# Gradient factors with all tokens in one row, one transposing load per block, key and value spectra in one load, and a new order

## The chip, the cores and the metric

The kernel runs on one core of a Trainium2 chip. The metric is device time in microseconds, the median of repeated executions. A separate execution was recorded by the profiler; its rows are what the text quotes. Engines are named as the profile names them: PE is TensorE's matmuls, PEld its weight loads, DVE is VectorE, ACT is ScalarE, POOL is GpSimd, and SP (SPq) is SyncE, which issues nearly all of the DMAs here.

## The reference

What is computed is the output of a block and all of its gradients. The input `q` (2048 tokens, 512 features, bf16) is normalised per token; the normalised rows feed two branches that are multiplied and added to the input.

```python
def _A_ref(q, k, v, shift_k, ssm_k, ssm_D):      # 4-tap shift, gate, long convolution by FFT
    for t in range(ks):
        k_shift = k_shift + k_pad[:, t:t + S, :] * shift_k[:, ks - 1 - t][None, None, :]
    kv = k_shift * v
    y = irfft(rfft(pad(kv)) * rfft(pad(ssm_k)))[:S] + kv * ssm_D
    return q * y

def _B_ref(x, w_gate, w_up, w_down):             # gated unit, F = 1376
    h = _sigmoid(x @ w_gate) * (x @ w_up)
    return h @ w_down

xn = _layernorm(A_q)
out = A_q + _A_ref(xn, ...) * _silu(_B_ref(xn, ...))
# returned: out, and the vjp with grad_out for q, k, v, shift_k, ssm_k, ssm_D, w_gate, w_up, w_down
```

(The FFT line is shortened to its meaning.) The outputs are `out_0` (the result), `out_1` to `out_6` (gradients of q, k, v, shift_k, ssm_k, ssm_D) and `out_7` to `out_9` (gradients of w_gate, w_up, w_down).

## The kernel before, in words

All data is bf16 with sums in f32. Tokens are cut into 16 tiles of 128 (`NJ`), taken in 8 pairs (`NP`); features into 4 groups of 128 (`NG`); the hidden size is padded to 11 blocks of 128 (`NFB`). The transforms of length 4096 are matmuls with tables (`step1`, `flip`, `step2` forward, `inv2`, `inv1` back), so a spectrum is a tile of 128 x 2048.

The work consists of generators, called streams here. The forward ones normalise (`f_ln`), compute gate and up products (`strG`), the spectra of the filter (`strK`) and of the gated input (`strV`, `strX`), and the rest of the gated unit (`strZ`). `strD` computes the gradient of the hidden layer. Three factors that the weight gradients need go to device memory on the way, through the helper `fm`: `hD` (the hidden layer h), `dgD` and `duD` (the gradients at the gate and up products), each stored feature by feature with tokens along the row. The spectra of the filter and of the gated input go to `KD` and `VD`, one 128 x 2048 tile for each group and half.

In the last part three streams run together. `dW` makes the weight gradients in 18 blocks: for each of the three factors, five blocks of 256 hidden features and one of 96. A block's operand is a tile `L` of 128 x 16 x 256 (token within a tile, tile, feature), read back from device memory by a transposing DMA in `ld_L`. Three such tiles take turns (`L_r`): after a block has been computed, `ld_L` asks for the block three further on. `frontC` and `backC` carry the gradient back through the convolution; `ld_KV` brings the two spectra in again, which `backC` multiplies by the gradient's spectrum, and the next two are asked for at the same place, so two pairs of tiles take turns. `last_rows` writes the two smallest gradients from a corner of one of these tiles.

Nothing is issued as the streams produce it. A recorder (`Rec`) collects all operations with a number each, and `emit` issues them in an order written out by hand: the table `ORDER` has one list of numbers for each engine's queue and one, `moves`, for the order of the DMAs over all queues, and `BANKS` says which PSUM banks each accumulator takes. As all operations pass through one line of `emit`, the profile shows line L524 for all of them, and they are told apart by engine, operation, tile name and shape. Buffers in SBUF come from one slab (`Arena`, `Ring`), so the profile calls every SBUF operand `slab`; the names of device memory (`KD`, `VD`, `hD`, `dgD`, `duD`) stay visible. A DMA in SP's queue waits there until what it reads is written and what it overwrites has been read, and everything behind it in that queue waits too.

Of the kernel before, what the change touches and what calls it, by code (L numbers as in the profile page):

```python
# [12 lines left out]
bf16 = mybir.dt.bfloat16  # L13
# [3 lines left out]
P = 128  # L17
NFFT = 4096
SCALE_INV = 2.0 / NFFT
S = 2048  # L20
# [3 lines left out]
NJ = 16  # L24
NFB = 11
LN_EPS = 1e-5
NG = 4
GW = D // NG
# [622 lines left out]
def kernel_impl(ctx, tc, A_q, A_k, A_v, A_shift_k, A_ssm_k, A_ssm_D, B_x, B_w_gate, B_w_up, B_w_down,  # L651
                grad_out, out_0, out_1, out_2, out_3, out_4, out_5, out_6, out_7, out_8, out_9):
    nc = tc.nc
# [12 lines left out]
    def fm(dst, p):  # L666
        o = 256 * (p % 4)
        return dst[p // 4][:, :, o:o + 256].rearrange("f p t -> p f t")
# [3 lines left out]
    ar = Arena(slab, SLAB)  # L672
# [879 lines left out]
```

## Time and profile before

| | |
|---|---|
| median of 3 runs | 447.37 us (446.88 to 447.51) |
| profiled execution | 446.62 us |
| its span in the profile | 444.3 us |
| PE busy | 433.5 us (98%), 4,871 matmuls recorded |
| DVE busy | 409.9 us (92%) |
| ACT busy | 279.8 us (63%) |
| POOL busy | 21.8 us (5%) |
| granted TensorE clock, mean | 0.997 |
| DMA moved | 116.85 MB, 263 GB/s on average |

Times within the span count from its start. Busy time is not work at full rate: matmuls overlap, so the mean length of one (the ns in the groups) is more than what it adds to a run of them; for that the busy time of a group is divided by its count. A DMA has two times: how long the issuing engine was occupied, and when its last byte landed. Rows with an arrow say what an engine waited for; the name behind the arrow is the releaser that came last. In rows of SPq the time is SP's own.

### The profile page before, as it was taken

How to read it: one execution, taken by the hardware profiler on the slowest of the kernel's cores; microseconds unless marked ns; L12 is line 12 of the kernel's file. 1: busy time of each engine (PE TensorE's matmuls, PEld its weight loads, DVE VectorE, ACT ScalarE, POOL GpSimd, SP SyncE). 2: the span in 40 equal slices, each digit the busy share in tenths (PEclk: the TensorE clock that was granted, in tenths of full speed). 3: DMA queues.
4: the chain of work that ended last, by engine and by line, in shares of the span. 5: the costliest groups of instructions: out<-in, count | busy, mean ns of one | idle time of the engine just before them, and what ended most of it. 6: DMA issues, size and time to landing. Idle time of an engine off the chain costs nothing.

```text
span 444.3 us, 11521 instructions
## 1 busy us (share of the span) xinstructions
PE 433.5 (98%) x4871; PEld 303.7 (68%) x4907; DVE 409.9 (92%) x630; ACT 279.8 (63%) x351; POOL 21.8 (5%) x48
## 2 busy tenths in 40 slices
PE   8999999999999999999999999999999999999994
PEld 3886686677868677655656655445577887887883
DVE  8899999999979898999999897899899999999991
ACT  7998878789777658786425333354556754656522
POOL 8301000001000000000000000000000000000000
PEclk9999999999999999999999999999999999999998
DMA  8999899779188999999899999799999999999998
GB/s 273 328 360 258 202 345 345 229 268 318 69 245 245 248 230 266 265 327 316 281 246 337 289 239 272 224 270 257 243 236 285 218 236 255 236 223 251 277 257 248
DMA packets 195813, 116.85 MB, mean 263 GB/s; under 512 B 107130, under 2 KB 182450, under 8 KB 195634
## 3 DMA queue, kind: packets, MB, share of 16 engines
q1 hardware_dynamic: 194688, 115.72, 99.2%
q8 instruction: 38, 0.62, 0.6%
q10 hardware_dynamic: 1074, 0.39, 0.3%
q14 instruction: 13, 0.11, 0.1%
HBM read 43.87 MB, written 46.70 MB: 204 GB/s over the span
## 4 chain that ended last, share of the span: by engine, by line
PE 94%; DVE 2%; issue 1%; DMA 1%; POOL 0%; ACT 0%; DVEq 0%
PE psum L524 94%; DVE slab L524 2%; DMA slab<-in_A_q_dram 1%; POOL slab L524 0%; ACT slab L524 0%; DVEq L524 0%
## 5 line engine op out<-in xcount | busy, mean ns | idle before, releaser
L524 PE MATMUL psum<-slab 128*128 128x256 bf16 (+5 forms) x4871 | 433.5, 299 | 4.6 <-DVE slab L524 1.9
L524 PEld LDWEIGHTS <-slab 128*128 128x128 bf16 (+2 forms) x4907 | 303.7, 96 | 134.2 <-issue 30.1
L524 ACT CAST slab<-psum 128x1024 bf16<-128x1024 f32 (+3 forms) x224 | 192.0, 897 | 128.6 <-PE psum L524 112.7
L524 DVE TENSOR_TENSOR slab<-slab 128x1024 bf16<-128x1024 bf16 (+4 forms) x302 | 239.9, 832 | 7.3 <-ACT slab L524 4.1
L524 DVE STREAM_TRANSPOSE slab<-slab 128x1024 f32<-128x1024 f32 x48 | 64.5, 1357 | 2.6 <-ACT slab L524 1.8
L524 ACT ACTIVATE slab<-slab 128x512 bf16<-128x512 bf16 (+5 forms) x59 | 49.5, 879 | 23.9 <-DVE slab L524 23.7
L524 DVE CAST slab<-psum 128x1024 bf16<-128x1024 f32 (+3 forms) x29 | 31.4, 1089 | 5.6 <-PE psum L524 5.2
L524 DVE TENSOR_TENSOR slab<-psum,slab 128x512 bf16<-128x512 f32 (+2 forms) x52 | 31.7, 610 | 3.4 <-PE psum L524 1.9
L524 ACT ACTIVATE slab<-psum 128x512 bf16<-128x512 f32 (+1 forms) x48 | 27.0, 575 | 2.0 <-PE psum L524 1.9
L524 POOL MEMSET slab<- 128x128 bf16 (+3 forms) x10 | 4.5, 453 | 273.1 <-PE psum L524 141.2
L524 DVE SCALAR_TENSOR_TENSOR slab<-slab 128x2 f32<-128x2 f32 (+2 forms) x41 | 14.3, 358 | 1.0 <-POOL slab L524 0.8
L524 POOL TENSOR_TENSOR slab<-slab 128x2 f32<-128x2 f32 (+3 forms) x11 | 11.1, 1016 | 77.5 <-DVE slab L524 77.4
L524 ACT ACT_TABLE_LOAD x10 | 12.8, 1283 | 1.9 <-issue 1.8
L524 DVE SCALAR_TENSOR_TENSOR slab<-psum,slab 128x512 bf16<-128x512 f32 x16 | 10.8, 684 | 3.3 <-PE psum L524 3.3
L524 DVE BATCH_NORM_STATS2 slab<-slab 128x6 f32<-128x512 bf16 x16 | 10.7, 677 | 0.9 <-DMA slab<-in_A_q_dram 0.9
L524 DVE STREAM_SHUFFLE slab<-slab 128x1024 f32<-128x1024 f32 x8 | 10.6, 1320 | 0.0
L524 ACT COPY slab<-psum 128x512 bf16<-128x512 bf16 (+2 forms) x10 | 7.4, 755 | 2.6 <-PE psum L524 2.6
L524 DVE TENSOR_SCALAR slab<-slab 128x512 bf16<-128x512 bf16 (+6 forms) x30 | 8.4, 299 | 0.1
L524 DVE COPY slab<-psum 128x512 bf16<-128x512 bf16 (+1 forms) x9 | 4.6, 526 | 0.2 <-PE psum L524 0.2
L524 POOL TENSOR_SCALAR slab<-slab 128x1 f32<-128x1 f32 (+3 forms) x10 | 3.3, 331 | 0.5
L524 DVE MEMSET slab<- 32x192 uint32 (+3 forms) x10 | 1.5, 160 | 1.3 <-PEq L1536 0.9
L524 DVE BATCH_NORM_AGGREGATE slab<-slab 128x2 f32<-128x6 f32 x16 | 2.5, 166 | 0.0
(14 smaller groups left out, 9.2 us busy)
## 6 DMA issues: line engine op xcount, KB each, us to landing
slab<-KD SPq DMA_DIRECT2D x16, 512.0 KB, 5.2
out_dram<-slab SPq DMA_DIRECT2D x31, 256.0 KB, 3.6
hD<-slab SPq DMA_DIRECT2D x8, 704.0 KB, 5.0
duD<-slab SPq DMA_DIRECT2D x8, 704.0 KB, 5.5
dgD<-slab SPq DMA_DIRECT2D x8, 704.0 KB, 5.2
slab<-in_A_k_dram SPq DMA_DIRECT2D x4, 1024.0 KB, 6.4
KD<-slab SPq DMA_DIRECT2D x8, 512.0 KB, 4.9
VD<-slab SPq DMA_DIRECT2D x8, 512.0 KB, 5.0
```

What stands on the lines that cost most here:

```text
L524: getattr(getattr(self.nc, eng), meth)(*[place(v) for v in a], **{x: place(v) for x, v in k.items()})
```

## The change

Three things change.

1. `hD`, `dgD` and `duD` were each two tensors of 11 x 128 x 1024 (feature block, feature, tokens of one half); each is now one of 11 x 128 x 2048. `ld_L` read a block by two transposing DMAs of 256 x 1024, one for each half of the tokens; it now reads it by one of 256 x 2048. 36 transposing loads of blocks become 18.
2. `KD` and `VD` become one tensor `KVD` with K and V side by side, 4 KB each, per partition. The two stores stay two, and `ld_KV` brings both in by one DMA of 128 x 4096 into one tile (`KV_r`). 16 loads become 8. The row-swapped read in `swap` takes the new pitch.
3. `ORDER` and `BANKS` are new tables: the recorder's numbers change with the removed DMAs (6,144 operations before, 6,118 now), and the order of the rest on every engine is another one. The set of matmuls, by shape and number, is the same.

```diff
-    KD = [dram.tile([2, P, 2048], bf16, name=f"KD{g}") for g in range(NG)]
-    VD = [dram.tile([2, P, 2048], bf16, name=f"VD{g}") for g in range(NG)]
+    KVD = [dram.tile([2, P, 2, 2048], bf16, name=f"KVD{g}") for g in range(NG)]
...
-    hD, dgD, duD = ([dram.tile([NFB, P, 1024], bf16, name=f"{t}{h}") for h in range(2)] for t in ("hD", "dgD", "duD"))
+    hD, dgD, duD = (dram.tile([NFB, P, S], bf16, name=t) for t in ("hD", "dgD", "duD"))
 
     def fm(dst, p):
-        o = 256 * (p % 4)
-        return dst[p // 4][:, :, o:o + 256].rearrange("f p t -> p f t")
+        return dst[:, :, 256 * p:256 * p + 256].rearrange("f p t -> p f t")
...
-                nc.sync.dma_start(KD[cg][q], KF)
+                nc.sync.dma_start(KVD[cg][q, :, 0], KF)
...
-            K = KD[n // 2][n % 2]
-            nc.sync.dma_start(KS, bass.AP(K.tensor, K.offset + 2048, [[4096, 64], [-2048, 2], [1, 2048]]))
+            K = KVD[n // 2][n % 2]
+            nc.sync.dma_start(KS, bass.AP(K.tensor, K.offset + 4096, [[8192, 64], [-4096, 2], [1, 2048]]))
...
-                nc.sync.dma_start(VD[cg][q], Xc)
+                nc.sync.dma_start(KVD[cg][q, :, 1], Xc)
...
         nb = 2 if u < 5 else 1
-        for h in range(2):
-            nc.sync.dma_start_transpose(L[:, 8 * h:8 * h + 8, 0:128 * nb], srcs[s][h][2 * u:2 * u + nb].rearrange("f p t -> (f p) t"))
+        nc.sync.dma_start_transpose(L[:, :, 0:128 * nb], srcs[s][2 * u:2 * u + nb].rearrange("f p t -> (f p) t"))
...
-            KK, VV = KK_r.next(), VV_r.next()
-            nc.sync.dma_start(KK, KD[cg][q])
-            nc.sync.dma_start(VV, VD[cg][q])
-            stC["KV", n] = KK, VV
+            KV = KV_r.next()
+            nc.sync.dma_start(KV, KVD[cg][q])
+            stC["KV", n] = KV[:, 0], KV[:, 1]
...
 ORDER = {
     "sync": """
...
-        5378 5597 5595 4775 5734 5234 5735 4576 5926 5733 4772 5925 5927 5965 5757 6006 6143 6075 5921 6008 6109 5825
-        5918
+        5710 5213 5572 5709 4561 5901 5900 4756 5732 5800 5980 5896 6049 6117 5982 6083 5939 5893
```

Three places show how the order moved. In its rows a name with an arrow is what an instruction writes and reads, a shape is that of what it writes, and a count at the end stands for equal neighbours. A transposing load of 128x8x256 is half a block, one of 128x16x256 a whole one; `slab<-in_A_k_dram` is the key's halves and their 3-row borders for the backward part.

First place: SP's queue in the last third, where blocks of `duD` are loaded beside the stores. Before:

```order
L524 DMA_TRANSPOSE slab<-duD_98 128x8x256
L524 DMA out_dram<-slab 128x4x256 x2
L524 DMA slab<-KD_64 128x2048
L524 DMA_TRANSPOSE slab<-duD_97 128x8x256
L524 DMA out_dram<-slab 128x2048
L524 DMA_TRANSPOSE slab<-duD_98 128x8x256
L524 DMA_TRANSPOSE slab<-duD_97 128x8x256
L524 DMA_TRANSPOSE slab<-duD_98 128x8x256
L524 DMA slab<-VD_68 128x2048
L524 DMA out_dram<-slab 128x4x96
L524 DMA_TRANSPOSE slab<-duD_97 128x8x256
```

and now:

```order
L520 DMA_TRANSPOSE slab<-duD 128x16x256
L520 DMA out_dram<-slab 128x2048
L520 DMA_TRANSPOSE slab<-duD 128x16x256
L520 DMA slab<-KVD_64 128x4096
L520 DMA out_dram<-slab 128x4x96
L520 DMA slab<-in_A_k_dram 15x3x256
L520 DMA out_dram<-slab 128x4x256
L520 DMA slab<-kshD_60 128x2048
L520 DMA_TRANSPOSE slab<-duD 128x16x256
```

The halves of a block, which had stores or a spectrum between some of them, are one row; K and V, which stood six rows apart, are one row behind a block's load.

Second place: VectorE in the head, where the first pair of token tiles is normalised. `TENSOR_SCALAR` of 128x512 scales one tile of 128 tokens; `BN_STATS` (in the profile BATCH_NORM_STATS2) belongs to later tiles; the copies bring transposed tiles out of PSUM. Before:

```order
L524 TENSOR_SCALAR slab<-slab 128x512
L524 BN_STATS slab<-slab 128x6
L524 SCALAR_TENSOR_TENSOR slab<-slab 128x1
L524 COPY slab<-psum 128x1024
L524 TENSOR_SCALAR slab<-slab 128x512
L524 COPY slab<-psum 128x512
L524 COPY slab<-psum 128x1024
L524 COPY slab<-psum 128x512
L524 TENSOR_TENSOR slab<-slab 1x128
L524 BN_STATS slab<-slab 128x6 x3
```

and now:

```order
L520 TENSOR_SCALAR slab<-slab 128x512
L520 SCALAR_TENSOR_TENSOR slab<-slab 128x1
L520 TENSOR_SCALAR slab<-slab 128x512
L520 COPY slab<-psum 128x1024
L520 COPY slab<-psum 128x512
L520 COPY slab<-psum 128x1024
L520 COPY slab<-psum 128x512
L520 TENSOR_TENSOR slab<-slab 1x128
L520 BN_STATS slab<-slab 128x6 x4
```

One BN_STATS and one copy of 1,024 went from ahead of the second scaling to behind it; the BN_STATS now stands with three others behind the copies.

Third place: the end of SP's queue, the last stores. `128x2048` is a group of the filter's gradient (`out_5`), `128x8x256` half of the tokens of two groups of the key's gradient (`out_2`), `128x2x96` and `128x4x256` are weight gradients, `4x128` and `4x512` the two smallest outputs. Before:

```order
L524 DMA out_dram<-slab 128x8x256
L524 DMA out_dram<-slab 128x2x96
L524 DMA out_dram<-slab 128x4x256
L524 DMA out_dram<-slab 4x128
L524 DMA out_dram<-slab 128x4x256
L524 DMA out_dram<-slab 128x2x96
L524 DMA out_dram<-slab 128x2048
L524 DMA out_dram<-slab 4x512
```

and now:

```order
L520 DMA out_dram<-slab 128x2048
L520 DMA out_dram<-slab 128x8x256
L520 DMA out_dram<-slab 4x128
L520 DMA out_dram<-slab 128x4x256
L520 DMA out_dram<-slab 128x2x96
L520 DMA out_dram<-slab 128x4x256
L520 DMA out_dram<-slab 128x2x96
L520 DMA out_dram<-slab 128x8x256
L520 DMA out_dram<-slab 4x512
```

The store of the filter's gradient went ahead of the last weight gradients, and half of the key's gradient took its place behind the last of them.

More of the change, by code (lines that the diff above doesn't have):

```diff
@@ L33 @@
     "tensor": """
[62 rows of a table removed]
[61 rows of a table added]
     """,
     "vector": """
[25 rows of a table removed]
[25 rows of a table added]
     """,
     "scalar": """
[15 rows of a table removed]
[15 rows of a table added]
     """,
     "gpsimd": """
-        56+1 29 87 30 63 92 88 38 34 89 98 91 86 99 90 117 100+1 118 103+2 107+1 106 109 81 110 144 102 119 111+1 229
-        503 937 914 1328 1659 1931 2263 3543 4774
+        56+1 29 87 63 30 38 34 98+1 81 90 86 89 88 100 118 92 101 103 117 91 104 102 105+2 111 110 144 108 112 109 229
+        503 119 937 914 1328 1931 1659 2263 3538 4758
     """,
     "sync": """
[11 rows of a table removed]
[10 rows of a table added]
     """,
     "moves": """
[12 rows of a table removed]
[10 rows of a table added]
     """,
@@ L173 @@
 BANKS = (
-    "33300311012220003001211110100010000101120000101000011101011001031001032011100001100001013101011002011011001011"
-    "00001111100021010101010100100101010001000110101001101000101101032102101012310101321003101032101231010110023001"
-    "01011100021210100101020211003211232011020220221302321121202210211012013222223331021223102102122301120231010301"
-    "21031001012102330301321"
+    "32013102320313331001121110100010000101100300101000011101011001001001323011100001100001013101011002011011001001"
+    "00001111100021010101010100100101010011000110101001101001100132032131101012321101301003101003101321010110023101"
+    "01011100021210101201021221213012230001202220212302321121000210201012013200210331020223102010220312120331010301"
+    "21031001013102220301231"
 )
@@ L1282, in kernel_impl @@
     late = ((Ring, [NJ + 3, 2 * GW], 1), (Ring, [NJ, 2 * GW], 1), (WRing, 2048, 1), (WRing, 2048, 1), (Ring, [NJ + 3, GW], 1),
-            (Ring, [2048], 2), (Ring, [2048], 2), (Ring, [2048], 2), (WRing, 1024, 1), (Ring, [NJ, GW], 1), (Ring, [128, NJ], 1),
+            (Ring, [2, 2048], 2), (Ring, [2048], 2), (WRing, 1024, 1), (Ring, [NJ, GW], 1), (Ring, [128, NJ], 1),
             (Ring, [NJ, GW], 1), (Ring, [256], 1))
@@ L1464, in last_rows @@
     def last_rows():
-        row4, row6 = (v[:, a:b] for v, a, b in zip(2 * [VV_r.next()], (0, 512), (512, 640)))
+        row4, row6 = (v[:, a:b] for v, a, b in zip(2 * [KV_r.next()[:, 1]], (0, 512), (512, 640)))
         for lag in range(4):
@@ L1484, in kernel_impl @@
         r.free()
-    kh_r, vg_r, B1_r, B2_r, dks_r, KK_r, VV_r, Y_r, Bq_r, ksh_r, dKT_r, term_r, dm_r = ar.rings(
+    kh_r, vg_r, B1_r, B2_r, dks_r, KV_r, Y_r, Bq_r, ksh_r, dKT_r, term_r, dm_r = ar.rings(
         *late)
```

243 rows, old and new, of the table ORDER are left out of this document.

## The prediction

> **What bounds the kernel now.** I read four views in this order: busy time by stretch, costliest groups by shape, waits, and the chain that ended last. The first is cut where the head ends (17.4 us), where the last uninterrupted run of matmuls begins (326) and where TensorE stops (438.2). The columns are the stretch, its length, then busy time of PE, PEld, DVE, ACT and POOL, granted clock, DMA share, GB/s.
>
> ```profile
> 0.00:17.40 17.40, 15.27 (x133) 9.70 (x134) 14.70 (x45) 13.74 (x17) 13.43 (x38) 1.00 0.91 293
> 17.40:326.00 308.60, 306.27 (x2914) 200.79 (x2949) 288.73 (x470) 203.67 (x255) 7.61 (x9) 1.00 0.96 267
> 326.00:438.20 112.20, 112.00 (x1829) 93.17 (x1828) 106.47 (x118) 61.82 (x80) 0.73 (x1) 1.00 1.14 253
> 438.20:444.30 6.10, 0.00 (x0) 0.00 (x0) 0.00 (x0) 0.57 (x1) 0.00 (x0) 0.75 0.56 173
> 326.58 111.59 PE psum L524 x1808
> 438.20 0.57 ACT slab L524
> PE psum L524 <- DVE slab L524: 1.9, 2, 1.3
> PE psum L524 <- issue: 0.8, 5, 0.2
> PEld L524 <- issue: 30.1, 110, 0.4
> DVE slab L524 <- DMA slab<-KD: 1.1, 1, 1.1
> ```
>
> TensorE is busy 306.27 of 308.60 us in the middle and 112.00 of 112.20 in the last third; lines five and six are the end of the chain of waits, 1,808 matmuls in a row and one copy. The waits (last four lines: engine, releaser, us in all, times, longest) leave next to nothing that is not matmul, and no DMA is among the releasers of PE. What isn't TensorE is 17.40 − 15.27 = 2.1 us in the head, 2.3 + 0.2 in the middle and 6.1 behind the last matmul, under 11 us of a span of 444.3. VectorE is second (288.73 of 308.60) and follows closely, and the DMA engines are full throughout.
>
> The matmul prices come from the groups by shape (count, busy, mean ns of one, idle before):
>
> ```profile
> L524 PE MATMUL psum<-slab 128*128 128x256 bf16 x1696 | 214.0, 273 | 0.7 <-issue 0.2
> L524 PE MATMUL psum<-slab 128*128 128x128 bf16 x872 | 71.6, 219 | 0.9 <-DVE slab L524 0.7
> L524 PE MATMUL psum<-slab 32*32 32x512 bf16 x1168 | 29.0, 381 | 0.1
> L524 PE MATMUL psum<-slab 128*32 128x128 bf16 x256 | 4.9, 220 | 0.0
> ```
>
> Matmuls overlap, so the price of one in a row is the busy time over the count: 214.0/1696 = 0.126 us for 128x256, 71.6/872 = 0.082, 29.0/1168 = 0.025 and 4.9/256 = 0.019.
>
> **The change, part by part.** *Matmuls.* The new order has the same matmuls in every shape, so the term on TensorE's 433.5 us is 0; only the order among them differs, and a different order costs what it makes TensorE wait.
>
> *Fewer DMA issues.* 18 transposing loads and 8 K/V loads go away. Their issuer waits most of the time (its own waits, same columns), so freed issue time alone is worth 0:
>
> ```profile
> SPq L524 <- PE psum L524: 99.3, 42, 7.0
> SPq L524 <- DVE slab L524: 97.6, 40, 7.3
> SPq L524 <- ACT slab L524: 33.6, 22, 12.5
> L524 SPq DMA_TRANSPOSE slab<-duD x12: 1764/3638/6408, 370.9 to 427.9; - x12
> DMA to landing us min/median/max: 4.5/6.7/8.7
> L524 SPq DMA_TRANSPOSE slab<-dgD x12: 1239/3129/4334, 312.1 to 369.1; - x12
> L524 SPq DMA_DIRECT2D slab<-KD x16: 325/522/1079, 49.7 to 381.9; - x16
> L524 SPq DMA_DIRECT2D slab<-VD x8: 351/492/2622, 286.6 to 396.1; - x8
> DMA to landing us min/median/max: 2.9/5.5/9.9
> 387.35 8.66 SPq L524 DMA_TRANSPOSE slab<-duD  x3
> 397.22 4.44 SPq L524 DMA_TRANSPOSE slab<-duD  x1
> ```
>
> 99.3 + 97.6 + 33.6 = 230.5 us of waiting for work that isn't finished. If that cover were gone, the most to win is 18 times the smallest issue, 18 × 1.2 = 22 us of SP's time, and none of it is TensorE's.
>
> *One transposing load per block of weight gradients.* The trace has no load of this size. Each half occupies SP for 1.764 to 6.408 us, median 3.638 (fourth line), and lands 6.7 us after its start (median, fifth), so 6.7 − 3.6 = 3.1 us after its issue ends. A whole block is bounded below by two short issues, 2 × 1.8 + 3.1 = 6.6 us, and by two median ones above, 2 × 3.6 + 3.1 = 10.4; three halves back to back took 8.66 us (second line from the end), 2.9 each, which gives 2 × 2.9 + 3.1 = 8.9. I take 8.9, because that row has halves issued in a row, as the merged one has them. What hides it: three buffers take turns, so a load may run from the last matmul that reads the old block to the first that reads the new one. Counting the instructions between these two in the new order, the tightest case holds 54 matmuls 128x256, 36 128x128, 32 32x512 and 64 of 128x32 weights: 54 × 0.126 + 36 × 0.082 + 32 × 0.025 + 64 × 0.019 = 11.8 us; the next ones hold 12.0, 12.5 and 12.6. So the load is hidden with 11.8 − 8.9 = 2.9 us to spare, the term is 0; where the cover is gone, all that is over is TensorE's, and a load of the two longest issues, 2 × 6.4 + 3.1 = 15.9, would be 4.1 over. The cover is thin because SP must also be free: behind such a load stand the stores, the K/V load and the next block's load, as the first piece of the order shows, and blocks of weight gradients wait for these.
>
> *K and V in one load.* Eight loads of K and eight of V, 512 KB each, become eight of 1 MB, with 8 KB in a row per partition. Landing of such a half takes 2.9 to 9.9 us, median 5.5. The product with K, which was free to start when K was in, now waits for V too. Bounds: 0, when both are there long before, to 1.1 + 0.5 = 1.6 us (the one wait for K that there is, plus one more issue of 0.5) at the first product; later ones are asked for two products ahead. That wait would be VectorE's, TensorE runs weight gradients meanwhile, and the new order puts no more of VectorE's work ahead of that product than the old one: I take 0.
>
> *The head.* One BATCH_NORM_STATS2 and one copy out of PSUM of 1,024 go from ahead of the second normalised half to behind it (the DVE rows of the order). The first four rows are VectorE's, the last two TensorE's.
>
> ```profile
> 7.40 0.69 DVE L524 BATCH_NORM_STATS2 slab<-slab 128x6 f32<-128x512 bf16 x1
> 8.07 0.68 DVE L524 COPY slab<-psum 128x1024 bf16<-128x1024 bf16 x1
> 8.68 0.40 DVE L524 TENSOR_SCALAR slab<-slab 128x512 bf16<-128x512 bf16 x1
> 9.00 1.34 DVE L524 COPY slab<-psum 128x512 bf16<-128x512 bf16 x3
> 1.26 5.62 PE L524 MATMUL psum<-slab 128*128 128x512 bf16 x24 [1.26 <-DVE slab L524]
> 7.55 4.66 PE L524 MATMUL psum<-slab 128*128 128x128 bf16 x50 [0.67 <-DVE slab L524]
> ```
>
> The scaled half (8.68) comes 0.69 + 0.68 − 0.1 (they overlap a little) = 1.3 us earlier, but the copies of its transposed tiles come behind the moved copy again, so TensorE gets less than that. The lower bound is TensorE's idle time in the head without what passes before its first matmul, 2.1 − 1.26 = 0.9, so −0.9. The upper bound is that a later cast, which now has a fourth BATCH_NORM_STATS2 ahead of it (0.69), holds TensorE up for all of it, and that the first matmul comes later by a MEMSET or two that now stand ahead (0.1 each): +0.9. I take −0.4, about half of what there is to win, because the row that is nearest (0.67 of waiting for VectorE at 7.55) is a wait of just this kind.
>
> *The tail.* The last large store is half of the key gradient, 512 KB in rows of 512 bytes, instead of 512 KB in rows of 4 KB, both right behind the last weight gradient.
>
> ```profile
> 429.86 9.80 SPq L524 DMA_DIRECT2D out_dram<-slab  x10
> out_dram<-slab SPq DMA_DIRECT2D x3, 512.0 KB, 5.1
> out_dram<-slab SPq DMA_DIRECT2D x2, 48.0 KB, 4.3
> ```
>
> The first row is the last ten stores, issued until 439.66; the others are the stores of the last 20 us, with the median time from issue to landing: 5.1 us for the three of 512 KB (two of them with rows of 512 bytes), 4.3 for the two small ones. If the length of the rows doesn't matter, the change is 0; if the rows of 512 bytes cost as much more as a 512 KB store costs beyond a 48 KB one, it is 5.1 − 4.3 = +0.8. I take +0.3, nearer to 0, because the three share one median.
>
> Sum: 0 + 0 + 0 + 0 − 0.4 + 0.3 = −0.1 us. The profiled execution took 446.62 us (span 444.3 and 2.3 around it), so the changed one would take 446.5; the median of the runs, 447.37, is 0.75 above the profiled one, which makes **447.3 us**: no change. About 0.2%, 0.9 us, is what can be told from no change here.
>
> **Rivals.** *A, faster, 446.1.* The head gives all it can, the tail costs nothing, and the new order loses some waits in the middle, 0.4 of the 2.3 us there: 447.37 − 0.9 − 0.4 = 446.1. For it: TensorE waits for VectorE in single waits of up to 1.3 us, and an order can take away one such. Against it: the middle's 2.3 us lie in many places. The Trainium skill ("DMA: Bandwidth & Descriptors", "Rules for kernel authors") asks to coalesce many small transfers into large ones and for 1 MiB per DMA; by that rule this case would come out as A. The DMA share of 0.96 to 1.14 agrees that the engines are full; PE's waits, which name no DMA, speak against a gain from emptier ones.
>
> *B, slower, about 449.* The merged load is late. A block's first matmul, which needed the first half only, now waits for all 16 token rows. Place: the last third, in the 11.8 to 12.6 us windows. It decides when a load needs more than the window, that is when SP reaches it 11.8 − 8.9 = 2.9 us late, or a load takes as long as the two longest issues. For it: SP's queue holds stores that wait up to 12.5 us for ACT ahead of loads; against it: the median sum of 8.9. Price: one load at the upper 10.4 that SP starts 2.4 us late misses its window by 10.4 + 2.4 − 11.8 = 1.0, and two of them make 2.0: 447.3 + 2.0 = 449.3; one alone gives 448.3. The Trainium skill ("DMA: Bandwidth & Descriptors", "Two DMAs through the same engine are not ordered") has it that data has landed once the semaphore's full increment has arrived, so that one load frees its users only as a whole; in this trace each half has its own start and landing.
>
> *C, slower, 448.4.* The first K/V product waits for the whole 1 MB and TensorE has nothing left to put in its place: +1.1.
>
> *D, the change doesn't do what it says.* The merged load occupies SP and the DMA engines as two halves in a row would and both orders keep TensorE as busy as it is: head and tail stay, and the time is 447.37.
>
> **How the numbers follow.** The forecast 0.36, A 0.33, B 0.21, C 0.07, D 0.03. Faster by over 0.2% is A, 0.33; within 0.2% the forecast and D, 0.39; slower B and C, 0.28. The forecast's own range is 446.5 to 448.2. The range of 8 in 10 reaches into A as far as the bounds of the head and one lost wait go (447.37 − 0.9 − 0.6 = 445.9) and into B to its two late loads, 449.3.
>
> **What would show it.** In the changed profile: PE busy near 433.5; the transposing loads 18 in number, with an issue of 5 to 7 us if merging saves nothing and under 4 if it does; no `PE psum <- DMA` row if the windows hold, and B if there is one with 1 us or more. The stretch to 17.4 us holds 0.4 more of the same matmuls; the stretch behind the last matmul is 6.1 to 6.9 us. A wait of DVE for the K/V load above 1.1 us speaks for C only if PE waits for DVE there. The forecast is wrong if TensorE's last matmul ends more than 0.9 us from where it ended, or if the tail alone moves by that much.

## The result, and the profile after

| | before | changed |
|---|---|---|
| median | 447.12 us (446.88 to 447.51, 4 runs) | 455.18 us (453.59 to 455.58, 4 runs) |
| profiled execution, its span | 446.62, 444.3 us | 453.59, 451.7 us |
| ratio, 95% interval | | 1.0173 (1.0147 to 1.0199) |

The change made the kernel 8 us slower. The forecast was 447.3 with a range of 445.9 to 449.3. The profiled execution of the changed kernel is its quickest; the other three had a lower mean granted clock (0.989 or 0.990 instead of 0.995), which matters below.

The page of the changed kernel: busy times, granted clock in tenths by slice, and the chain by engine.

```profile
PE 436.2 (97%) x4871; PEld 304.8 (67%) x4907; DVE 412.4 (91%) x632; ACT 279.7 (62%) x349; POOL 21.6 (5%) x48
...
PEclk9989999999999999999999999999999999999999
...
PE 87%; DMA 5%; ACT 3%; DVE 3%; issue 1%; ACTq 0%; DVEq 0%
```

The waits of its TensorE:

```profile
PE psum L520 <- DMA slab<-in_B_w_up_dram: 4.4, 1, 4.4
...
PE psum L520 <- DMA slab<-in_B_w_gate_dram: 0.9, 1, 0.9
```

and the two pieces of its chain that are transfers (start, length):

```profile
21.67 10.04 DMA slab<-in_B_w_up_dram
...
166.67 11.06 DMA slab<-in_B_w_gate_dram
```

Before, no DMA released TensorE; now two do, and neither is a load that the change merged. One wait of 4.4 us is for `in_B_w_up_dram`, a weight of the forward part, 30 us into the kernel. TensorE's stretches there, in the changed kernel (columns as in the prediction):

```profile
18.00:26.00 8.00, 8.00 (x101) 7.01 (x100) 7.70 (x13) 7.40 (x10) 0.00 (x0) 1.00 1.05 331
26.00:32.00 6.00, 1.60 (x19) 1.21 (x18) 2.97 (x4) 2.64 (x4) 0.00 (x0) 0.93 1.09 362
32.00:37.00 5.00, 5.00 (x56) 3.89 (x55) 2.64 (x4) 2.21 (x3) 0.00 (x0) 0.74 1.05 326
```

The start of the third stretch, microsecond by microsecond:

```profile
31.75:32.75 1.00, 1.00 (x5) 0.72 (x6) 0.00 (x0) 0.00 (x0) 0.00 (x0) 0.50 0.92 393
...
33.75:34.75 1.00, 1.00 (x11) 0.92 (x10) 1.00 (x2) 0.22 (x1) 0.00 (x0) 0.59 1.09 464
34.75:35.75 1.00, 1.00 (x15) 0.93 (x13) 1.00 (x2) 1.00 (x2) 0.00 (x0) 1.00 1.46 265
```

and in the kernel before:

```profile
26.00:32.00 6.00, 6.00 (x76) 5.10 (x75) 6.00 (x8) 5.75 (x10) 0.00 (x0) 1.00 1.08 398
32.00:37.00 5.00, 4.95 (x57) 3.44 (x56) 5.00 (x9) 4.30 (x6) 0.73 (x1) 1.00 1.10 283
```

After the wait the granted clock is 0.50 for two microseconds and 0.59 in the third: TensorE is "busy", but at half its rate. So the wait costs more than it lasts.

Who issues that load? Not SP. The weights w_gate and w_up are fetched in three pieces; the first 256 columns of w_up come from ScalarE's queue. Its rows in the changed kernel:

```profile
16.65 0.60 ACT L520 ACTIVATE slab<-psum 128x512 bf16<-128x512 f32 x1
...
21.22 0.60 ACT L520 ACTIVATE slab<-psum 128x512 bf16<-128x512 f32 x1
21.67 0.38 ACTq L520 DMA_DIRECT2D slab<-in_B_w_up_dram  x1
```

SP's rows there:

```profile
20.47 0.43 SPq L520 DMA_DIRECT2D slab<-in_B_w_down_dram  x1
20.94 1.07 SPq L520 DMA_DIRECT2D slab<-in_A_q_dram  x1
```

and the load in the table of its DMAs (issuer, size, time from issue to landing):

```profile
slab<-in_B_w_up_dram ACTq DMA_DIRECT2D x1, 256.0 KB, 10.0
```

In the kernel before, ScalarE's row and the same table:

```profile
16.07 0.37 ACTq L524 DMA_DIRECT2D slab<-in_B_w_up_dram  x1
```

```profile
slab<-in_B_w_up_dram ACTq DMA_DIRECT2D x1, 256.0 KB, 5.5
```

The new table puts this one DMA behind five more of ScalarE's operations (the first experiment's expectation below counts four): 5.6 us later. By then SP has sent for w_down (1,280 KB) and for pairs of q tiles, and a load of 256 KB that took 5.5 us takes 10.0.

Where the 7.4 us of span are, worked out from when the matmuls of both kernels start, against the same amount of matmul work at full rate: 0.7 in the first 26 us, 4.6 in this wait, 1.2 in the slow stretch behind it, 1.0 at 172 to 178 us (the wait for w_gate's transposing load), 0.4 scattered over the rest, −0.5 behind the last matmul (5.6 us instead of 6.1). The 0.4 can't be placed, as the mean price of a matmul is too coarse for that. From 320 us on, where most of the merged loads are, TensorE's waits are 0.6 us in all (0.2 before), none of them for a DMA.

### The profile page after: what moved, and what is told of

The parts are those of the page before. It is cut to its first block, busy times and chain, and to the rows that moved or that the text cites. A ratio compares the mean times of both kernels' runs of the same rounds, so it can differ in the third digit from the quotient of the medians.

```text
span 451.7 us, 11484 instructions
## 1 busy us (share of the span) xinstructions
PE 436.2 (97%) x4871; PEld 304.8 (67%) x4907; DVE 412.4 (91%) x632; ACT 279.7 (62%) x349; POOL 21.6 (5%) x48
## 4 chain that ended last, share of the span: by engine, by line
PE 87%; DMA 5%; ACT 3%; DVE 3%; issue 1%; ACTq 0%; DVEq 0%
PE psum L520 87%; DVE slab L520 3%; ACT slab L520 3%; DMA slab<-in_B_w_gate_dram 2%; DMA slab<-in_B_w_up_dram 2%; ACT L520 0%; ACTq L520 0%; DVEq L520 0%
## 5 line engine op out<-in xcount | busy, mean ns | idle before, releaser
L520 ACT CAST slab<-psum 128x1024 bf16<-128x1024 f32 (+2 forms) x224 | 192.1, 897 | 141.8 <-PE psum L520 116.0
L520 DVE TENSOR_TENSOR slab<-slab 128x2048 bf16<-128x2048 bf16 (+4 forms) x302 | 240.5, 831 | 7.0 <-ACT slab L520 4.2
L520 DVE CAST slab<-psum 128x1024 bf16<-128x1024 f32 (+4 forms) x29 | 31.3, 1085 | 10.3 <-ACT slab L520 6.6
L520 DVE TENSOR_SCALAR slab<-slab 128x512 bf16<-128x512 bf16 (+6 forms) x31 | 11.2, 376 | 0.3
L520 ACT COPY slab<-psum 128x1024 bf16<-128x1024 bf16 (+2 forms) x9 | 7.2, 826 | 2.6 <-PE psum L520 2.6
```

The costliest lines, as they stand in the source:

```text
L520: getattr(getattr(self.nc, eng), meth)(*[place(v) for v in a], **{x: place(v) for x, v in k.items()})
```

## The experiments

The first theory after the result: the late piece of w_up and the slow clock behind it are the loss. Its rival is rival B of the prediction, the merged loads. All ratios are to the kernel before on the same chip (its medians there: 446.34, 447.08 and 446.89 us for the three groups of four). The lists in the cuts of code are shortened; where a DMA moves, the list `moves` is changed to match.

| | ratio | 95% interval | median, us |
|---|---|---|---|
| changed, w_up early | 1.0033 | 1.0016 to 1.0050 | 447.62 |
| before, w_up later | 1.0016 | 0.9996 to 1.0037 | 447.02 |
| changed, loads split | 1.0318 | 1.0288 to 1.0347 | 460.58 |
| before, loads merged at the later half | 1.0345 | 1.0314 to 1.0376 | 461.88 |
| before, w_up later by one more step | 1.0120 | 1.0092 to 1.0148 | 452.71 |
| changed, w_up and w_gate early | 1.0012 | 0.9993 to 1.0030 | 447.57 |
| the same, identity first ("mended") | 1.0004 | 0.9987 to 1.0020 | 447.28 |
| before, loads merged at the earlier half | 1.0440 | 1.0404 to 1.0477 | 466.60 |
| mended, a gradient load behind two others | 0.9992 | 0.9976 to 1.0008 | 446.59 |
| mended, transposing loads split | 1.0094 | 1.0069 to 1.0119 | 451.39 |
| mended, K/V loads split | 1.0021 | 0.9993 to 1.0049 | 447.17 |
| changed, w_down later | 1.0144 | 1.0118 to 1.0170 | 453.72 |

### The late piece of w_up

The changed kernel with the load (operation 3) where the kernel before has it:

```diff
 "scalar": ... 
-        329 253 309 320 281 114 292 194 412 3 543
+        329 253 309 320 3 281 114 292 194 412 543
```

> The changed kernel with one instruction moved: ScalarE issues the load of the first 256 columns of w_up where the kernel before does, right behind its first activation out of PSUM, instead of four steps later. Theory 1 (late weight piece): the load goes out at 16 to 17 us instead of 21.7 and lands before TensorE asks for it at 27.3, so the wait of 4.4 us goes, and the stretch at a granted clock of 0.74 behind it (about 1.3 us): 455.2 - 5.7 = 449.5, with TensorE's row of waiting for in_B_w_up_dram gone. Theory 2 (the merged transposing loads or merged K/V loads make it slower): within 1 us of 455.2.

Measured 1.0033, 447.62 us, from 1.0173: over 6 us are gone. The load goes out at 15.5 us and lands 7.0 us later, no wait for it is left, and the clock stays up. Of the 1.5 us that remain, 1.1 can be the wait for w_gate's load, which is as long as that in its profile. Theory 1 holds; the merged loads, all still in, are not the cause.

The other way round, the kernel before with the load moved behind ScalarE's copy at 21 us:

```diff
 "scalar": ...
-        309 253 320 3 281 114 292 194 440 543
+        309 253 320 281 114 292 194 440 3 543
```

> The kernel before with the same load moved the other way, behind ScalarE's copy of 1,024 at 21.6 us. Theory 1: issued at about 22.0 and 10 us to landing behind 3.3 MB of other loads, so it lands near 32 and TensorE, which asks at 25.8, waits 5 to 6 us, then runs about 1.3 us longer at a lower clock: 447.1 + 7 = 454, with a wait for in_B_w_up_dram. Theory 2: 447.1, no change.

This missed: 1.0016, no difference that can be told. The load went out at 20.76 us, 4.7 later than before, landed in 4.6 us, at 25.4, and nobody waited. So the late issue alone is not it. In this kernel SP sends for w_down at 21.12 us, just behind the load:

```profile
20.76 0.42 ACTq L524 DMA_DIRECT2D slab<-in_B_w_up_dram  x1
21.12 0.44 SPq L524 DMA_DIRECT2D slab<-in_B_w_down_dram  x1
slab<-in_B_w_up_dram ACTq DMA_DIRECT2D x1, 256.0 KB, 4.6
```

In the changed one w_down goes out at 20.47, ahead of it. The sharper theory: what counts is the transfers that stand ahead of a load when it is issued. One more step back puts it behind them:

```diff
-        309 253 320 281 114 292 194 440 3 543
+        309 253 320 281 114 292 194 440 543 3
```

> The kernel before with ScalarE's load of w_up moved one step further than in the run before, behind the activation at 22.5 us, so that it goes out behind SP's loads of w_down (1.3 MB, 21.2), v (2 MB, 22.05) and q (22.7). Theory 1 in its sharper form (not the late issue alone but the transfers that are ahead of it by then): issued at 23, landing 9 to 10 us later, 32.5; TensorE, which asks at about 27, waits 5 us and then runs slower for some us: 446.4 + 6.5 = 453, with a granted clock under 0.9 for 5 us behind the wait. If the issue time alone counts, each us later costs one: 20.8 cost nothing, so 23 costs 1 to 2 us, 448.

Measured 1.0120, 452.71. The load was issued at 21.70, 0.94 us later than in the experiment above and now behind w_down, and TensorE got it at 30.57, 5.2 us later than it landed there. SP's and ScalarE's rows, the wait, and the stretch behind it in this kernel:

```profile
21.19 0.43 SPq L524 DMA_DIRECT2D slab<-in_B_w_down_dram  x1
21.70 0.41 ACTq L524 DMA_DIRECT2D slab<-in_B_w_up_dram  x1
```

```profile
PE psum L524 <- DMA slab<-in_B_w_up_dram: 3.8, 1, 3.8
```

```profile
30.57:31.57 1.00, 1.00 (x11) 0.91 (x12) 0.00 (x0) 0.00 (x0) 0.00 (x0) 1.00 1.10 442
```

The expected slow clock did not show in the profiled execution (1.00 right after the wait of 3.8 us); its span is 4.7 above that of the kernel before. The other three executions had a mean clock of 0.990 to 0.992 instead of 0.996 and took 1.1 to 2.6 us more, which a slow stretch in them would explain; they have no profile that shows where.

Last, the changed kernel with the load as late as it is, and less ahead of it:

```diff
 "sync": ...
-        84 2 507 233 79 148 470 80 85 120
+        84 2 148 470 80 85 507 233 79 120
```

> The changed kernel with ScalarE's load of w_up as late as it is there (21.7 us), but SP's loads of w_down (1.3 MB) and of two pairs of q tiles, used from 40 us on, put behind that of v, so that less is ahead of it. If the 10.0 us to landing come from the transfers ahead: landing in 5 to 6 us, at 27 to 28, a wait of 0 to 1 us and no lowered clock: 447.5 to 449. If the late issue alone is to blame: still 455.

Half of it came true. With the same issue time the load landed in 4.5 us instead of 10.0, and the wait for it is gone. But the kernel stayed at 1.0144: w_down (operation 79), now behind v's 2 MB and ahead of a transposing load of 15 us, took 14.1 us to land and became the next thing that TensorE waits for, and this wait was followed by the longest slow stretch of all. Its table of DMAs, its waits, its chain and stretches around and behind the wait:

```profile
slab<-in_B_w_up_dram ACTq DMA_DIRECT2D x1, 256.0 KB, 4.5
```

```profile
PE psum L520 <- DMA slab<-in_B_w_down_dram: 3.8, 1, 3.8
```

```profile
23.98 14.14 DMA slab<-in_B_w_down_dram
```

```profile
37.00:42.00 5.00, 3.62 (x15) 1.94 (x17) 4.40 (x10) 0.00 (x0) 2.11 (x2) 0.54 1.05 274
42.17:43.17 1.00, 1.00 (x11) 0.94 (x9) 0.00 (x0) 0.89 (x1) 0.00 (x0) 0.50 0.93 372
```

The clock was 0.50 in each microsecond from 38.17, where the wait of 3.84 us ended, to 43.17, and 0.72 from there to 45: about 3 us lost beside the wait. From 18 to 42 us the DMA engines are full (a share of 0.91 to 1.30 by stretches), and the transfer that was put off was late itself: TensorE asked for w_down at 34.3 us, 10.3 us after the issue.

### The merged loads, in both orders

The changed kernel with its order, every merged load issued as two halves in a row (`f` is the call of the first line):

```diff
-        getattr(getattr(self.nc, eng), meth)(*[place(v) for v in a], **{x: place(v) for x, v in k.items()})
+        if meth == "dma_start_transpose" and tuple(a[1].shape)[-1] == S:
+            for h in range(2):
+                f(a[0][:, 8 * h:8 * h + 8], a[1][:, 1024 * h:1024 * h + 1024])
+        elif meth == "dma_start" and tuple(a[0].shape) == (P, 2, 2048):
+            for h in range(2):
+                f(a[0][:, h], a[1][:, h])
+        else: ...
```

> The changed kernel with its new order, but each merged transposing load issued as two halves in a row, and each K/V load as two. Theory 1: within 1 us of 455.2, as none of them is waited for. Theory 2: most of the 8 us comes back, 447 to 449.

Neither: 460.58, by the ratios 6.5 us slower still. The wait for w_up is there as before (4.7 us), and VectorE now waits 4.2 us for `KVD`; the two splits are taken apart below. And the kernel before with its order, the two halves of a block as one load at the later half's place:

```diff
+                    if op.mate is not None:
+                        if not op.mate.seen:        # the earlier half: nothing is issued here
+                            ...
+                        ...
+                        op.alts = [(op.alts[0][0], op.alts[0][1], op.whole, {})]
```

> The kernel before with its old order and the unified factors in device memory, the two halves of each transposing load issued as one load at the place of the later half; K and V stay apart. Theory 1: within 1 us of 447.1, at most 1 more where a first half used to be early. Theory 2: 449 to 455, with TensorE waiting for hD, dgD or duD.

461.88, 15.5 us slower: here theory 2's numbers came, and TensorE waited as rival B had it. The earlier half's place, wherever the old order allows it (all but one block), is no better:

> The kernel before with merged transposing loads as in the merged run, but each at the place of the earlier half (the first one of hD, which can't stand there, at the later). If the 15 us were due to the later place: within 2 us of 446.4. If they are due to a whole block having to be free and to SP being occupied 5 to 6 us in a row: still 455 or more, with SP waiting longer for PE and stores and K/V loads late behind it.

466.60, worse than at the later half's place. In the first of the two, TensorE's waits, the stretch of the one for `hD`, and SP's queue ahead of it:

```profile
PE psum L533 <- DMA slab<-duD: 5.8, 4, 2.7
...
PE psum L533 <- DMA slab<-hD: 5.5, 1, 5.5
```

```profile
275.00:285.00 10.00, 5.68 (x22) 2.42 (x23) 1.49 (x5) 0.00 (x0) 0.00 (x0) 0.66 1.14 270
```

```profile
253.96 10.02 SPq L533 DMA_DIRECT2D duD<-slab  x2
264.16 5.41 SPq L533 DMA_TRANSPOSE slab<-hD  x1
```

and the waits of the second:

```profile
PE psum L544 <- DMA slab<-hD: 9.7, 2, 8.5
...
DVE slab L544 <- DMA slab<-VD: 2.8, 1, 2.8
```

In the kernel before, the first half of `hD` is asked for at 246.8 us (the first start in its tile row, 246.8 to 307.6), in its short gaps between stores. As one load it goes out at 264.2, behind two stores, the second of which SP has issued at 264.0, and the first weight gradient waits 5.5 us. The wait, which ends at 279.3 us, is again followed by a low clock (0.66 in the row, 0.50 from 280 to 283 us). So under the old order the merge costs 15 us, and under the new one it does not: there TensorE waits for none of these blocks, and the first load of `hD` goes out at 201 us. The merged loads and the new order belong together.

What the merge is worth in the new order shows with the head mended (below). Transposing loads split, K/V whole:

> The mended changed kernel (w_up early, w_gate's load and identity first), its transposing loads of whole blocks issued as two halves in a row, K and V still in one. If merging saves SP's time (6.1 us for a whole block against 2 x 3.5) and the new order needs that: 2 to 4 us slower than the mended one, 449.5 to 451. If merging saves nothing in this order: 447.3.

K/V split, transposing loads whole:

> The same mended kernel with the transposing loads whole and each K/V load issued as two. If the K/V merge is what the last third lives on (VectorE waited 4.2 us for these loads when both were split): 449 to 451. If it is worth only the one issue of 0.5 us that it saves: 447.3 to 447.8.

1.0094 and 1.0021, against 1.0004 for the mended kernel itself. The K/V merge is worth nothing that can be told, the transposing one about 4 us. SP's queue near 390 us with halves, in pairs:

```profile
383.45 6.97 SPq L524 DMA_TRANSPOSE slab<-duD  x2
...
391.61 7.74 SPq L524 DMA_TRANSPOSE slab<-duD  x2
399.44 0.53 SPq L526 DMA_DIRECT2D slab<-KVD  x1
```

with the waits that follow,

```profile
DVE slab L526 <- DMA slab<-KVD: 5.3, 3, 3.8
PE psum L526 <- DVE slab L526: 4.9, 3, 3.1
```

and in the mended kernel with whole loads:

```profile
382.94 5.00 SPq L520 DMA_TRANSPOSE slab<-duD  x1
...
388.66 5.04 SPq L520 DMA_TRANSPOSE slab<-duD  x1
393.79 0.53 SPq L520 DMA_DIRECT2D slab<-KVD  x1
```

A whole block occupies SP for 5.0 us where two halves take 7.0 to 7.7. Two blocks stand ahead of the K/V load, so with halves it goes out 5.65 us later; VectorE waits 3.8 us for it and TensorE 3.1 for VectorE.

### What is left when the head is mended

Three more moves were tried on top of "w_up early". First, w_gate's transposing load (2478) ahead of three small loads in SP's queue:

```diff
-        1941 2270 1944 2265 2476 2267 2478 2484
+        1941 2270 1944 2478 2265 2476 2267 2484
```

> The changed kernel with w_up early, and SP's transposing load of w_gate (ready when TensorE's last product with the old weights is done) put ahead of three small loads that aren't used for 10 us. Theory: it is issued 1.0 us earlier and the wait of TensorE for it (1.1 us) goes: 447.6 - 1.1 = 446.5, level with the kernel before. Rival: it waits in the queue for the last product anyway and lands as late, 447.6.

1.0012 (from 1.0033). No wait for w_gate is left, as expected; the gain in time is within the two intervals. Second, the identity ahead of GpSimd's long product:

```diff
 "gpsimd":
-        56+1 29 87 63 30 38
+        56+1 29 87 30 63 38
```

> As the run before, and GpSimd makes the identity ahead of its long product of 1,024 integers, as the kernel before does. Theory: the head's 0.7 us (4.45 against 3.75 us lost by 26 us) comes from the transposes that wait for the identity and from VectorE's scalar operations that run beside the long product: 0.5 to 0.7 off, 445.9. Rival: it is the order of VectorE and of the q loads, and nothing changes, 446.5.

1.0004. In its profile the first 26 us lose 3.5 us instead of 4.45; the ratio's interval doesn't tell it from the one before. Third, a load of a gradient tile (2740) behind two loads that are needed sooner:

```diff
-        2740 2703 2326 2440
+        2703 2326 2740 2440
```

> The changed kernel with w_up early, w_gate's transposing load and the identity first, and besides SP's load of a gradient tile that is used 20 us later put behind a transposing load and a load of q that are waited for at 184 us. Theory: the wait of 0.8 us behind it goes, 447.2 - 0.8 = 446.4 on the scale of the last comparison, a little under the kernel before (0.998). Rival: the next late thing takes its place, 1.000.

0.9992 (0.9976 to 1.0008). Expected was 0.998, or 1.000 if another late thing takes its place: the interval holds both. The mended kernel is level with the one before; none of these versions beats it by more than can be measured.

## Why the prediction was wrong

**The bound.** TensorE bounds the kernel before and after, and with under 11 us of idle time little was to be won: right. That the same idle time says nothing of what can be lost was not drawn from it.

**The head: the step that failed.** Its term of −0.4 and its bounds, −0.9 to +0.9, came from VectorE's and TensorE's rows around 8 us and ended there. Measured: +0.7 up to 26 us, then +4.6 and +1.2, 6.5 us where the sum had −0.4. The order of ScalarE was not read at all, although it issues one of the weight loads and the change moved that by five operations. The working also priced SP's DMAs only; a DMA that a compute engine issues has to be priced too. The prediction's own rows would have told that it matters: the DMA share of 0.91 in the head says that transfers queue up, and ScalarE's row in the profile before had the price, 5.5 us from 16.07, for a product that asks at about 27 us. Issued 5.6 us later, with 1.3 MB more ahead, the load takes an estimated 3.6 to 4 us more to land for the bytes of w_down alone, at the 330 to 360 GB/s of those stretches. The 1.0 us at 172 to 178 us is of the same kind: the order of the loads in the middle was put at 0 without a look at which load now goes out later.

The Trainium skill, page "DMA: Bandwidth & Descriptors", section "Issuing engines are not separate DMA queues", says that DMAs of scalar, sync and gpsimd end up on the same 16 DMA engines and interleave. The runs agree: ScalarE's load landed in 4.5 to 10.0 us, by what SP had issued ahead of it.

**The head's sign.** The forecast of −0.4 for the earlier second half was wrong by itself too: the first 26 us lost 0.7 more. The step read VectorE's rows from 7.4 us on, and the loss starts at 2.5. In the changed kernel GpSimd's long product of 1,024 integers starts at 1.37 us, ahead of the identity, and a VectorE operation of 1,024 integers that starts beside it at 2.48 takes 2.27 us:

```profile
1.37 2.83 POOL L520 TENSOR_TENSOR slab<-slab 128x1024 int32<-128x1024 int32 x1
L520 DVE TENSOR_SCALAR slab<-slab 128x1024 int32<-128x1024 int32 x1 | 2.3, 2267 | 0.0
```

So it does in the version with w_up and w_gate early. With the identity first, the only thing in which the mended version differs from that one, GpSimd's product starts at 2.57, just behind VectorE's operation, which then takes 0.69 us (as in the kernel before):

```profile
2.57 2.96 POOL L520 TENSOR_TENSOR slab<-slab 128x1024 int32<-128x1024 int32 x2
L520 DVE TENSOR_SCALAR slab<-slab 128x1024 int32<-128x1024 int32 x1 | 0.7, 693 | 0.0
```

VectorE's first BATCH_NORM_STATS2 starts at 4.73 us in the one and at 3.78 in the other, and the run of matmuls that waits for VectorE at 9.22 and at 8.29. The identity itself is ready at 4.90 us in the changed kernel, long before that run.

**The merged transposing load.** Right for the kernel as it is: no wait for `hD`, `dgD` or `duD`, as the windows had it. The durations, from the tile row of the changed kernel:

```profile
L520 SPq DMA_TRANSPOSE slab<-duD x6: 5514/6104/7505, 378.5 to 426.2; - x6
DMA to landing us min/median/max: 3.9/7.4/11.2
```

The load landed 7.4 us after its start (median, with the stores of that tile; 8.9 taken, 6.6 to 10.4 as bounds), so the cover of 11.8 was enough. The test that was set for it was bad: "5 to 7 us if merging saves nothing". 6.1 us falls there, yet two halves of `duD` in a row, with the new order, take 7.0 to 9.1. "Fewer DMA issues" at 0 was too low in the same way. The 230.5 us of waiting that it rests on can't be: SP's DMA instructions before, added up from the trace, fill 303 of the 444.3 us, so at most 141 are left for waiting, and in the last third they fill 98 of 118. The rows of SP's waits therefore count time in which it was issuing. In that last third K/V loads queue up behind the blocks, and there the saved issue time is worth about 4 us. It does not show in the result because the kernel before, with halves, had an order that suits halves.

**Rival B** was given 0.21 for a late block. Its mechanism exists, with a price of 15 to 20 us in the old order, where it was priced at 2; in the new order no wait for a block is left. **Rival C** did not happen (VectorE waited 0.7 us for a K/V load), **rival D** neither, and **rival A** was not to be had: with the head mended the kernel is level.

**The tail.** Expected +0.3, measured −0.5 (6.1 to 5.6 us). It is small, and its cause was not tested.

**The clock.** It was not in the working. A wait of 4.4 us cost about 5.8, since the clock then ran at half. The executions with a mean clock of 0.989 to 0.990 took 1.4 to 2 us more than the profiled one, so this second term probably differs from one execution to the next; only one of them has a profile.

## What to carry to other kernels

When a change replaces a table of orders, list the DMAs of every engine's queue with their old and new issue time, those of compute engines too, and look at the first use of each. Here a load's time to land went with what had been sent for ahead of it, on either queue: moving one by a microsecond across a large transfer cost five, and putting the large one off made that one late. Test a data-movement change and its schedule apart before giving credit to either: here the merge under the old order cost 15 to 20 us, and the mended new order without the merged transposing loads about 4.

## What the runs showed of the hardware

A stop of TensorE near 4 us may or may not be followed by a slow clock. After 3.83 us in one run it was 1.00 at once; after 3.84 us in another it was 0.50 for five microseconds; after 4.4 us it was 0.50 for two and back at 1.00 after three. The Trainium skill, page "TensorE: Matmul & The Clock Gate", section "Part 1: The HAM clock gate (the "warmup" mystery)", has a free-running activity window of about 3.4 us, from which it follows that a stop somewhat longer than one window holds a whole idle one only if it falls right. The two outcomes near 3.8 us agree with that; the runs don't measure the window, and why the slow stretches differ in length stays open.

A VectorE TENSOR_SCALAR of 128x1024 int32 took 0.69 us when it started just ahead of GpSimd's product of the same size, and 2.27 us when it started 1.1 us behind the start of that product.

One transposing load of 1 MB occupied the issuing queue for about 5.0 us where two of half the size took 7.0 to 7.7 in the same place; over the first five blocks of `duD` in these two kernels it was 5.0 to 6.8 against 7.0 to 9.1. The rows of the halves before had suggested their sum.
